# The order of the values in the last batch of an attention kernel with gated experts

## The chip, the cores and the metric

The kernel runs on one core of a Trainium2 chip. The metric is the device time of one execution in microseconds; each version is run several times and the median counts. One execution is also profiled, and from its trace come all the times of single instructions below.

## The reference

Two blocks follow one another. The first is a linear attention on features: for 4 batches, 4 heads, 1088 positions and 32 dimensions it makes 64 features of each key and query and divides a weighted sum of values by a sum of weights. Its result x (4 x 1088 x 128) goes to the second block, which holds nearly all of the time: four experts, each a causal softmax attention with a head of 64, of which every position takes the two with the largest gate.

```python
logits = x @ w_gate                      # top 2 of 4 experts, weights w
for e in range(E):                       # E = 4
    q = x @ wq[e]; k = x @ wk[e]; v = x @ wv[e]          # 1088 x 64
    scores = scale * (q @ k.transpose(0, 2, 1))          # causal mask
    a = np.exp(scores - scores.max(-1, keepdims=True))
    a /= a.sum(-1, keepdims=True) + 1e-09
    ye = a @ v @ wo[e]                                   # 1088 x 128
    out += mask[e] * w * ye
```

## The kernel before

The 1088 positions of a batch are nine tiles of 128 queries, the last of 64. The four experts are two groups g of two (e = 0, 1). One **unit** of work is one tile i of one group, and goes through these steps:

- `scores` (L416, L422): PE multiplies the queries of the tile with all keys up to it, for both experts, into PSUM banks of the pool `ps_sc`. It holds two tiles of two banks each; a tile over 512 columns wide takes one of them for each expert.
- DVE takes the maximum of each row (`mx`, L426 for tiles up to 512 columns, L429 else), ACT the exponential with the sum of the row (`soften`, L402), which writes `a` in SBUF. `a` has four buffers, so a pair of tiles with two experts fills them.
- `turns_of` (L476): PE transposes `a` in blocks of 128 by 128, up to four in a PSUM bank `tp`, and `evacuate` copies the bank to `aT` in SBUF (L72 on ACT, every third one L70 on DVE). The pool `ps_tp` has four banks, which all small products share.
- Two neighbouring tiles of a group are one pair p, with 256 queries. When both are turned, `values` (L546) multiplies `aT` with the values `vt`, block by block of keys (j), one product for each j and expert (two matmul instructions each in the trace), into one bank `av`.
- `gates` makes 1/sum times the gate weight (`r` on DVE L496 and L497, `rb` on POOL L500) and returns `turn`, which transposes `rb` on PE into the other half of the bank `av` (L506) and copies it to `rs` (L508, ACT). DVE multiplies the two (`yT`, L548).
- `output` (L599): PE multiplies `yT` of both groups with `wo`, a copy makes `ob`, and SP issues the output DMA (L604).

`units` yields the units of a batch, with their kind: "A" and "B" for the first and the second tile of a pair, "P" for a pair taken as one unit (both scores first, then all turns), "L" for the last tile of 64 queries. In the last batch (b = B - 1) the pairs come from the largest to the smallest, p = 3, 2, 1, 0, with the L unit behind p = 3; p = 1 is of kind P there, and p = 0 of kinds A and B.

PE's order is the order in which the program writes its instructions (`manual_schedule`); on the other engines a scheduler sets the order. For each unit the main loop writes: the scores (`make`); the values of an older group if one is `ready`; the jobs, which are the turns left over by the unit before and an output; and, for kinds A and B with more than two turns, the first half of its own turns. A group is ready one unit after it was closed:

```python
ready = len(groups) > (1 if kind != "L" and closed else 0)
```

So the values of a group stand behind the scores of a later unit. In batches 0 to 2 work of the next batch (`fill`) is spread between the jobs; the last batch has none. After the last unit come the turns left over, the values of the last group (p = 0, g = 1) with its gate, and the last output.

Of the kernel before, what the change touches and what calls it, by code (L numbers as in the profile page):

```python
# [10 lines left out]
F32 = mybir.dt.float32  # L11
BF16 = mybir.dt.bfloat16
I32 = mybir.dt.int32
ALU = mybir.AluOpType
# [5 lines left out]
def kernel(  # L20
# [20 lines left out]
    nc = tc.nc  # L41
    B, H, S, D = q.shape
    R = S1.shape[0]
    DM, E = w_gate.shape
    HD = wq.shape[2]
# [4 lines left out]
    NG = E // 2  # L50
# [73 lines left out]
    if NS == 2:  # L124
# [15 lines left out]
        def both(o, x, y, op):  # L140
            nc.vector.tensor_tensor(out=o, in0=x, in1=y, op=op)
# [326 lines left out]
    def turns_of(name, i, ats, aT, q0):  # L468

        def some(e0, e1, j0, j1):  # L470
            tp = ps_tp.tile([128, 512], F32, tag="tp", name=f"tp{name}_{e0}_{j0}")
            nk, nj = size(j0), j1 - j0
            for e in range(e0, e1):
                for j in range(j0, j1):
                    x = 128 * (nj * (e - e0) + j - j0)
                    nc.tensor.transpose(tp[0:nk, x : x + 128], ats[e][:, 128 * j : 128 * j + nk], ident)  # L476
            evacuate(aT[0:nk, e0:e1, j0:j1, q0 : q0 + 128],
                     tp[0:nk, 0 : 128 * nj * (e1 - e0)].rearrange("p (e j s) -> p e j s", e=e1 - e0, j=nj))

        n = min(i + 1, NJ - 1)  # L480
        if n <= 2:
            cuts = [(0, 2, 0, n)]
        elif n <= 4:
            cuts = [(0, 1, 0, n), (1, 2, 0, n)]
        elif n <= 6:
            cuts = [(0, 1, 0, 4), (0, 2, 4, n), (1, 2, 0, 4)]
        else:
            cuts = [(0, 1, 0, 4), (0, 1, 4, n), (1, 2, 0, 4), (1, 2, 4, n)]
        if i == NJ - 1:
            cuts.append((0, 2, n, NJ))  # L490
        return [lambda c=c: some(*c) for c in cuts]

    def gates(name, z, gws, w):

        r = p4.tile([128, w // 128, 2], F32, tag="r", name=f"r{name}")
        nc.vector.tensor_scalar_add(r, z, 1e-9)  # L496
        nc.vector.reciprocal(r, r)  # L497
        rb = p4.tile([128, 2, 128], F32, tag="rb", name=f"rb{name}", bufs=2)
        wide = [128, w // 128, 2, HD]
        nc.gpsimd.tensor_tensor(out=rb[:, 0 : w // 128].rearrange("p x (e d) -> p x e d", d=HD),  # L500
                                in0=gws[:, :, :, None].to_broadcast(wide), in1=r[:, :, :, None].to_broadcast(wide),
                                op=ALU.mult)

        def turn(t):
            for x in range(w // 128):
                nc.tensor.transpose(t[:, 128 * x : 128 * x + 128], rb[:, x], ident)  # L506
            rs = p4.tile([128, 256], F32, tag="rs", name=f"rs{name}", bufs=2)
            nc.scalar.copy(rs[:, 0:w], t[:, 0:w])  # L508
            return rs

        return turn
# [5 lines left out]
    def spend(us):  # L517

        debt[0] += us
        while fill and debt[0] >= fill[0][0] / 2:  # L520
            cost, f = fill.popleft()
            debt[0] -= cost
            f()
# [4 lines left out]
    def units(b, qk, vt, gw, gw8):  # L528


        for p in range((NJ - 1) // 2) if b < B - 1 else reversed(range((NJ - 1) // 2)):
            yT = p2.tile([128, NG, 256], F32, tag="yT", name=f"yT{b}_{p}")
            nk = 2 * (2 * p + 2)
            for g in range(NG):
                aT = p2.tile([128, 16 * 256], F32, tag="aT", name=f"aT{b}_{p}_{g}")
                aT = aT[:, 0 : nk * 256].rearrange("p (e j s) -> p e j s", e=2, s=256)
                z = p4.tile([128, 2, 2], F32, tag="z", name=f"z{b}_{p}_{g}")
                name = f"{b}_{p}_{g}"

                def values(to_gate, p=p, g=g, aT=aT, yT=yT, name=name):  # L540
                    av = ps_tp.tile([128, 512], F32, tag="tp", name=f"av{name}")
                    for j in range(2 * p + 2):
                        lo = 128 * max(0, j - 2 * p)
                        for e in range(2):
                            c = HD * (2 * g + e)
                            nc.tensor.matmul(av[HD * e : HD * e + HD, lo:256], vt[:, j, c : c + HD],  # L546
                                             aT[:, e, j, lo:256], start=(j == 0), stop=(j == 2 * p + 1))
                    nc.vector.tensor_tensor(out=yT[:, g], in0=av[:, 0:256], in1=to_gate(av[:, 256:]), op=ALU.mult)  # L548
                    return (lambda: output(b, p, yT)) if g == NG - 1 else None

                def close(p=p, g=g, z=z, name=name, values=values):
                    return gates(name, z, gw[:, 2 * p : 2 * p + 2, 2 * g : 2 * g + 2], 256), values

                def both(g=g, z=z, p=p):
                    return [scores(b, 2 * p + x, g, qk, z[:, x]) for x in range(2)]

                def turns(made, p=p, aT=aT, name=name):
                    return [f for x in range(2) for f in turns_of(f"{name}_{x}", 2 * p + x, made[x], aT, 128 * x)]

                if p == 1 or p == 0 and b < B - 1:  # L560
                    yield "P", both, turns, close
                    continue
                for x in range(2):
                    i = 2 * p + x
                    yield ("AB"[x], lambda i=i, g=g, z=z, x=x: scores(b, i, g, qk, z[:, x]),
                           lambda ats, i=i, aT=aT, x=x, name=name: turns_of(f"{name}_{x}", i, ats, aT, 128 * x),
                           close if x else None)
            if p == NJ // 2 - 1:
                yield last_unit(b, qk, vt, gw8)
# [37 lines left out]
    with tc.manual_schedule(engines={mybir.EngineType.PE}):  # L607

        warm = ps_tp.tile([128, 512], F32, tag="tp", name="warm")
        for _ in range(16):  # L610
            nc.tensor.matmul(warm[:, 0:128], idle, idle, start=True, stop=True)
        now, ahead, _, own = prepare(0)
        for _, f in ahead:
            f()

        turns, groups, closed, done = [], collections.deque(), False, None
        for b in range(B):
            if b + 1 < B:

                coming, ahead, mid, rest = prepare(b + 1)  # L620
                own, tail = own[:-5], own[-5:]
                lead = sum(c for c, _ in own)
                if b == 0:
                    own += tail
                    own += sum(ahead, [])
                else:
                    for f, o in zip(ahead, (tail[0:1], tail[1:2], tail[2:3], tail[3:])):
                        own += f + o
                fill.extend(own + mid)
                share = (sum(c for c, _ in fill) - lead) / sum(STEPS)  # L630
            for n, (kind, make, turned, close) in enumerate(units(b, *now)):
                jobs, turns = turns, []
                if done:
                    jobs.append(done)
                    done = None
                if kind == "L":
                    for f in jobs:
                        f()
                    jobs = []

                ready = len(groups) > (1 if kind != "L" and closed else 0)
                made = make()
                if ready:
                    to_gate, values = groups.popleft()
                    done = values(to_gate)
                us = share * STEPS[n] + (lead if n == 0 else 0.0) if b + 1 < B else 0.0
                gaps = max(len(jobs), 2)
                for s in range(gaps):
                    if s < len(jobs):
                        jobs[s]()  # L650
                    spend(us / gaps)
                turns = turned(made)
                if len(turns) > 2 and kind in "AB":
                    for f in turns[: len(turns) // 2]:
                        f()
                    turns = turns[len(turns) // 2 :]
                closed = close is not None
                if close:
                    groups.append(close())
            spend(1e9)  # L660
            debt[0] = 0.0
            now, own = coming, rest
        for f in turns + ([done] if done else []):
            f()
        for to_gate, values in groups:
            done = values(to_gate)
        done()
# [30 lines left out]
```

## Time and profile before

| | |
|---|---|
| median of 4 runs | 409.06 us (407.7 to 411.1) |
| profiled execution, its own time | 411.1 us |
| its span | 409.3 us |
| PE busy | 388.6 us, 95% of the span |
| DVE, ACT, POOL busy | 231.9, 224.1, 58.9 us |
| mean granted clock of PE | 0.992 |
| last batch, from its first scores | 317.25 us to the end |

The span is counted from the first instruction to the end of the last, with the last DMA. A line of the timeline gives the start, the time for which the instructions of the line were busy, engine and line of the code, the operation, the tiles out and in, their shapes and how many there were; what stands in brackets is the idle time of the engine before it and what ended it. PEld is the load of weights for a matmul. The chain that ended last gives start, length and what ran.

### The profile page before, as it was taken

The page shows a single profiled execution, that of the slowest core. Times are in us where ns is not written, and L with a number is a line of the kernel's source. Part 1 is how long each engine was busy: PE and PEld are TensorE (multiplying, and loading weights), DVE is VectorE, ACT ScalarE, POOL GpSimd, SP SyncE. Part 2 cuts the span into 40 slices and gives each one's busy share as a digit, 9 for nine tenths or more (in the row PEclk, how much of TensorE's full clock was granted, in tenths as well). Part 3 has the DMA queues.
Part 4 walks back from the last instruction along what each step waited for, and adds up shares of the span by engine and source line. Part 5 has one row for each costly group of instructions (what it writes and reads, how often), then busy time and mean ns, then how long its engine had stood idle before and what let it go on. Part 6 is the DMA issues. An engine that isn't in the chain of part 4 may idle for free.

```text
span 409.3 us, 8453 instructions
## 1 busy us (share of the span) xinstructions
PE 388.6 (95%) x3424; PEld 281.3 (69%) x3424; DVE 231.9 (57%) x501; ACT 224.1 (55%) x566; POOL 58.9 (14%) x92
## 2 busy tenths in 40 slices
PE   8899999999999999999999999999999989998895
PEld 8775787776748677776756778776665666675583
DVE  6877865565465564556446554645654555456332
ACT  2246565556555656556656466646654464656343
POOL 4400550000004340000002530000000000000100
PEclk9999999999999999999999999999999999999889
DMA  8604112000000000000000000000000000000000
GB/s 200 181 14 151 57 57 69 13 2 14 0 3 14 3 2 14 14 1 2 13 2 2 14 5 2 13 14 0 14 2 0 16 3 1 2 14 3 2 14 27
DMA packets 11351, 9.99 MB, mean 24 GB/s; under 512 B 3632, under 2 KB 10288, under 8 KB 11312
## 3 DMA queue, kind: packets, MB, share of 16 engines
q1 hardware_dynamic: 11296, 9.44, 8.3%
q8 instruction: 27, 0.44, 0.5%
q14 instruction: 12, 0.10, 0.1%
q10 hardware_dynamic: 16, 0.00, 0.0%
HBM read 7.22 MB, written 2.23 MB: 23 GB/s over the span
## 4 chain that ended last, share of the span: by engine, by line
PE 76%; DVE 11%; ACT 7%; issue 2%; DMA 1%; POOL 1%; SPq 0%; ACTq 0%; POOLq 0%
PE sc L416 17%; PE tp L476 16%; PE av L546 12%; PE qk L332 6%; ACT a L402 5%; PE po L599 4%; PE num L306 3%; PE vg L344 3%; PE av L584 3%; PE av L506 3%; DVE mx L458 2%; DVE mx L429 2%; PE sc L442 2%; PE kv L283 2%; PE tq L296 2%
## 5 line engine op out<-in xcount | busy, mean ns | idle before, releaser
L402 ACT ACTIVATE a<-sc,mx 128x1024 f32<-128x1024 f32 (+7 forms) x136 | 103.3, 765 | 72.4 <-DVE mx L429 47.2
L476 PE MATMUL tp<-ident,a 128*128 128x128 f32 (+1 forms) x648 | 92.7, 278 | 2.6 <-ACT a L402 1.4
L429 DVE TENSOR_REDUCE mx<-sc 128x1 f32<-128x640 f32 (+3 forms) x64 | 62.6, 1020 | 42.0 <-PE sc L422 42.0
L416 PE MATMUL sc<-qkT 64*128 64x512 f32 (+3 forms) x384 | 80.8, 519 | 2.2 <-ACT a L402 2.2
L476 PEld LDWEIGHTS tp<-ident,a 128*128 128x128 f32 (+1 forms) x648 | 74.0, 143 | 12.4 <-ACT a L402 3.0
L72 ACT COPY aT<-tp 128x512 f32<-128x512 f32 (+3 forms) x122 | 65.2, 553 | 30.1 <-PE tp L476 29.5
L546 PE MATMUL av<-aT,vt 128*64 128x256 f32 (+1 forms) x640 | 70.9, 369 | 2.3 <-ACT aT L72 2.3
L500 POOL TENSOR_TENSOR rb<-gw,r 128x256 f32<-128x256 f32 (+1 forms) x36 | 21.2, 590 | 305.0 <-DVE r L497 188.6
L546 PEld LDWEIGHTS av<-aT,vt 128*64 128x64 f32 x640 | 43.7, 139 | 23.5 <-ACT aT L72 2.7
L70 DVE COPY aT<-tp 128x512 f32<-128x512 f32 (+3 forms) x58 | 36.1, 624 | 34.5 <-PE tp L476 34.5
L416 PEld LDWEIGHTS sc<-qkT 64*128 64x128 f32 x384 | 33.8, 186 | 29.4 <-issue 21.6
L508 ACT COPY rs<-av 128x256 f32<-128x256 f32 (+1 forms) x36 | 13.0, 361 | 40.7 <-PE av L506 40.3
L332 PE MATMUL qk<-xT,wqk 128*128 128x512 f32 x64 | 31.4, 603 | 1.6 <-ACT a L402 1.6
L426 DVE TENSOR_REDUCE mx<-sc 128x2 f32<-128x256 f32 (+3 forms) x32 | 25.5, 816 | 7.6 <-PE sc L422 7.2
L402 ACT ACTIVATION_READ_ACCUMULATOR a<-sc,mx 128x1 f32 x136 | 27.3, 201 | 0.0
L422 PEld LDWEIGHTS <-mpick 64*128 64x128 bf16 x256 | 13.9, 95 | 17.4 <-issue 12.9
L599 PE MATMUL po<-wo,yT 128*128 128x128 f32 (+1 forms) x144 | 20.5, 282 | 1.9 <-DVE yT L548 0.8
L344 PE MATMUL vg<-wvg,xT 128*128 128x260 f32 (+1 forms) x72 | 20.3, 393 | 1.8 <-DVE r L496 0.6
L496 DVE TENSOR_SCALAR r<-z 128x4 f32<-128x4 f32 (+1 forms) x36 | 7.3, 204 | 23.9 <-ACT a L402 22.4
L72 ACT COPY qkT<-qk 128x512 f32<-128x512 f32 x23 | 13.5, 589 | 13.3 <-PE qk L332 13.0
L599 PEld LDWEIGHTS po<-wo,yT 128*128 128x128 f32 (+1 forms) x144 | 17.3, 185 | 4.4 <-DVE aT L70 1.3
L306 PE MATMUL num<-kvz,qpT 128*128 128x66 f32 x144 | 17.8, 272 | 0.6 <-ACT aT L72 0.3
(122 smaller groups left out, 412.7 us busy)
## 6 DMA issues: line engine op xcount, KB each, us to landing
kin<-in_k_dram SPq DMA_DIRECT2D x4, 544.0 KB, 3.9
qin<-in_q_dram SPq DMA_DIRECT2D x4, 544.0 KB, 6.0
vin<-in_v_dram SPq DMA_DIRECT2D x16, 128.0 KB, 5.5
out_dram<-ob SPq DMA_DIRECT2D x16, 128.0 KB, 1.8
vtl<-in_v_dram SPq DMA_DIRECT2D x8, 16.0 KB, 3.6
wqk<-in_moe_wq_dram SPq DMA_DIRECT2D x1, 128.0 KB, 5.0
wqk<-in_moe_wk_dram SPq DMA_DIRECT2D x1, 128.0 KB, 3.2
wvg<-in_moe_wv_dram SPq DMA_DIRECT2D x1, 128.0 KB, 3.1
```

What stands on the lines that cost most here:

```text
L70: nc.vector.tensor_copy(out_, in_)
L72: nc.scalar.copy(out_, in_)
L306: nc.tensor.matmul(num[:, 66 * (y - 2 * x0) : 66 * (y - 2 * x0) + 66], qpT[:, y], kvz[:, y % 2].rearrange("p h d -> p (h d)"), start=True, ...
L332: nc.tensor.matmul(t, wt(a), xT[:, 512 * c : 512 * c + 512], start=True, stop=True)
L344: nc.tensor.matmul(t[0:m, 0 : E * HD + E], xT[:, 128 * j : 128 * j + m], wvg, start=True, stop=True)
L402: nc.scalar.activation(out=dst, in_=src, func=ACTF.Exp, bias=mx, accum_out=z)
L416: nc.tensor.matmul(sc[e][:, c0:c1], qk[rows, g, 128 * i : 128 * i + 128], qk[rows, NG + g, c0:c1], start=True, stop=(c1 < n))
L426: nc.vector.tensor_reduce(mx, t[:, :, 0:n], axis=AX.X, op=ALU.max, negate=True)
L429: nc.vector.tensor_reduce(mx[:, e : e + 1], sc[e][:, 0:n], axis=AX.X, op=ALU.max, negate=True)
L476: nc.tensor.transpose(tp[0:nk, x : x + 128], ats[e][:, 128 * j : 128 * j + nk], ident)
L546: nc.tensor.matmul(av[HD * e : HD * e + HD, lo:256], vt[:, j, c : c + HD], aT[:, e, j, lo:256], start=(j == 0), stop=(j == 2 * p + 1))
L599: nc.tensor.matmul(po[0:nq, DM * x : DM * x + DM], yT[:, g, 128 * x : 128 * x + nq], wo_sb[:, g], start=(g == 0), stop=(g == NG - 1))
```

## The change

All of it is in the last batch. (1) For kinds A behind a B, the first half of the values (j up to p + 1) of the group just closed is written behind the jobs and ahead of the unit's own turns; the second half stands where all of them stood. This is so for the groups p = 3, g = 0 and p = 2, g = 0. (2) For kind P, the values of the group just closed, all of them, are written in the unit that follows it, behind the jobs, which are that group's last turns. (3) p = 0 becomes a pair of kind P too, and takes its tile 1 before its tile 0, in scores and turns. (4) For the last group `rb` is made on DVE instead of POOL, and the gate's transposes and `rs` are written ahead of the values.

```diff
-    def gates(name, z, gws, w):
+    def gates(name, z, gws, w, last=False):
...
-        nc.gpsimd.tensor_tensor(out=rb[:, 0 : w // 128].rearrange("p x (e d) -> p x e d", d=HD),
-                                in0=gws[:, :, :, None].to_broadcast(wide), in1=r[:, :, :, None].to_broadcast(wide),
-                                op=ALU.mult)
+        (nc.vector if last else nc.gpsimd).tensor_tensor(
+            out=rb[:, 0 : w // 128].rearrange("p x (e d) -> p x e d", d=HD),
+            in0=gws[:, :, :, None].to_broadcast(wide), in1=r[:, :, :, None].to_broadcast(wide), op=ALU.mult)
...
-                def values(to_gate, p=p, g=g, aT=aT, yT=yT, name=name):
-                    av = ps_tp.tile([128, 512], F32, tag="tp", name=f"av{name}")
-                    for j in range(2 * p + 2):
+                av = []
+
+                def some_values(j0, j1, p=p, g=g, aT=aT, name=name, av=av):
+                    if not av:
+                        av.append(ps_tp.tile([128, 512], F32, tag="tp", name=f"av{name}"))
+                    for j in range(j0, j1):
...
+                def values(to_gate, half=False, p=p, g=g, yT=yT, av=av, some_values=some_values):
+                    if half:
+                        return some_values(0, p + 1)
+                    if b == B - 1 and p == 0 and g == NG - 1:
+                        av.append(ps_tp.tile([128, 512], F32, tag="tp", name="av"))
+                        rs = to_gate(av[0][:, 256:])
+                        some_values(0, 2)
+                    else:
+                        some_values(p + 1 if av else 0, 2 * p + 2)
+                        rs = to_gate(av[0][:, 256:])
+                    nc.vector.tensor_tensor(out=yT[:, g], in0=av[0][:, 0:256], in1=rs, op=ALU.mult)
...
+                order = (1, 0) if b == B - 1 and p == 0 else (0, 1)
+
+                def both(g=g, z=z, p=p, order=order):
+                    return {x: scores(b, 2 * p + x, g, qk, z[:, x]) for x in order}
...
-                if p == 1 or p == 0 and b < B - 1:
+                if p <= 1:
                     yield "P", both, turns, close
...
+                if b == B - 1 and closed and kind in "AP" and n:
+                    to_gate, values = groups[-1]
+                    if kind == "P":
+                        groups.pop()
+                        done = values(to_gate)
+                    elif last_kind != "L":
+                        values(to_gate, half=True)
                 turns = turned(made)
...
-                closed = close is not None
+                closed, last_kind = close is not None, kind
```

More of the change, by code (lines that the diff above doesn't have):

```diff
@@ L545, in values @@
                             c = HD * (2 * g + e)
-                            nc.tensor.matmul(av[HD * e : HD * e + HD, lo:256], vt[:, j, c : c + HD],
+                            nc.tensor.matmul(av[0][HD * e : HD * e + HD, lo:256], vt[:, j, c : c + HD],
                                              aT[:, e, j, lo:256], start=(j == 0), stop=(j == 2 * p + 1))
-                    nc.vector.tensor_tensor(out=yT[:, g], in0=av[:, 0:256], in1=to_gate(av[:, 256:]), op=ALU.mult)
+                def values(to_gate, half=False, p=p, g=g, yT=yT, av=av, some_values=some_values):
[9 more added lines that the diff above has]
+                    nc.vector.tensor_tensor(out=yT[:, g], in0=av[0][:, 0:256], in1=rs, op=ALU.mult)
@@ L549, in values @@
                     return (lambda: output(b, p, yT)) if g == NG - 1 else None
                 def close(p=p, g=g, z=z, name=name, values=values):
[L552 to L558, printed above, removed]
@@ L560, in units, with turns @@
-                if p == 1 or p == 0 and b < B - 1:
+                    return gates(name, z, gw[:, 2 * p : 2 * p + 2, 2 * g : 2 * g + 2], 256,
+                                 b == B - 1 and p == 0 and g == NG - 1), values
+                order = (1, 0) if b == B - 1 and p == 0 else (0, 1)
+                def both(g=g, z=z, p=p, order=order):
+                    return {x: scores(b, 2 * p + x, g, qk, z[:, x]) for x in order}
+                def turns(made, p=p, aT=aT, name=name, order=order):
+                    return [f for x in order for f in turns_of(f"{name}_{x}", 2 * p + x, made[x], aT, 128 * x)]
```

## The prediction

> **What bounds the kernel now.** I read the page first (engine busy rows, clock row), then the busy time in stretches, the chain that ended last, and the timeline of the last batch. PE is busy 388.6 of 409.3 us and the chain is 76% PE, so a change of order can only win back PE's idle time and slow time. The edits touch only the last batch, which begins near 317 us. Busy time per stretch of 3.41 us (column two is length and PE's busy time, then PEld, DVE, ACT, POOL; then granted clock, DMA share, GB/s):
>
> ```profile
> 372.05:375.46 3.41, 3.41 (x31) 2.28 (x30) 2.86 (x6) 1.59 (x6) 0.61 (x1) 1.00 0.00 0
> 375.46:378.87 3.41, 1.72 (x14) 0.90 (x13) 1.85 (x4) 2.95 (x9) 0.00 (x0) 1.00 0.00 0
> 378.87:382.28 3.41, 3.41 (x18) 1.56 (x16) 1.25 (x2) 0.00 (x0) 0.61 (x1) 0.50 0.02 5
> ...
> 385.70:389.11 3.41, 1.70 (x20) 1.17 (x20) 1.39 (x4) 2.32 (x8) 0.61 (x1) 1.00 0.00 0
> 389.11:392.52 3.41, 3.41 (x21) 2.74 (x18) 0.42 (x1) 1.18 (x5) 0.00 (x0) 0.50 0.00 0
> ...
> 402.76:406.17 3.41, 2.40 (x18) 1.70 (x18) 0.43 (x1) 0.54 (x3) 0.17 (x1) 1.00 0.00 0
> ```
>
> Twice PE is idle for half of a stretch (1.72 and 1.70 us busy), and each time the granted clock is 0.50 for the next 3.41 us; with 2.40 us busy the clock kept 1.00. In a slow stretch the 24 values matmuls took 3.60 us against 2.60 at full clock, the four 512-wide scores 1.72 against 1.11, and 14 turns 2.55 against about 1.6. Each slow stretch costs 1.7 us: first 0.6 + 1.0 + 0.1; second 0.56 (16 values) + 0.25 (gate) + 0.95 (turns). What makes PE idle there:
>
> ```profile
> 375.99 1.07 ACT L72 COPY aT<-tp 128x512 f32<-128x512 f32 x2
> ...
> 376.15 0.92 PE L416 MATMUL sc<-qkT 64*128 64x384 f32 x4 [0.36 <-ACT a L402]
> ...
> 376.93 0.72 ACT L402 ACTIVATE a<-sc,mx 128x512 f32<-128x512 f32 x1
> ...
> 378.46 1.72 PE L416 MATMUL sc<-qkT 64*128 64x512 f32 x4 [1.34 <-ACT a L402]
> ...
> 384.59 0.58 ACT L402 ACTIVATE a<-sc,mx 128x384 f32<-128x384 f32 x1
> ...
> 387.05 0.98 ACT L72 COPY aT<-tp 128x384 f32<-128x384 f32 x2
> ...
> 388.08 2.29 PE L546 MATMUL av<-aT,vt 128*64 128x256 f32 x16 [1.65 <-ACT aT L72]
> ```
>
> The first stall is a score bank not yet read by ACT's exponentials; the second is the copy of turned tiles to aT, queued on ACT behind four exponentials. Those exponentials began only at 384.59, because a pair uses all four buffers of `a` and the turns that free them stood behind 24 values. The last chain:
>
> ```profile
> 402.82 0.87 PE av L546 x8
> 403.70 0.38 PE av L506 x2
> ...
> 404.15 0.38 ACT rs L508
> ...
> 404.56 0.44 DVE yT L548
> ...
> 405.04 0.95 PE po L599 x6
> ...
> 406.01 0.37 ACT ob L72
> ```
>
> After it 2.92 us pass until the span ends (the last output DMA).
>
> **Part 1: the halves.** For the groups p=3 g=0 and p=2 g=0, half of the values moves from behind the next scores to ahead of the next unit's own turns, where PE waits now:
>
> ```profile
> 332.54 1.09 PE L476 MATMUL tp<-ident,a 128*128 128x128 f32 x8
> ...
> 333.67 0.59 ACT L72 COPY aT<-tp 128x512 f32<-128x512 f32 x1 [2.20 <-PE tp L476]
> ...
> 334.64 0.68 DVE L70 COPY aT<-tp 128x512 f32<-128x512 f32 x1
> ...
> 335.31 0.98 PE L476 MATMUL tp<-ident,a 128*128 128x128 f32 x7 [1.09 <-ACT a L402]
> ```
>
> No instruction is added: 16 and 12 matmuls move. The half reads the block j 0 to 3, e=1, which is the first of the two tiles turned at 332.54. Its copy is the one on DVE, behind two maxima, and ends at 335.33. So the second matmul of the half waits until 335.35, the gap is not filled, and the half (16 at 1.67/16) ends near 336.95. Seven turns then reach 337.72, where the next scores begin (336.22 now): the softmax of tile 7 is 1.5 us late. PE has 1.67 us less to do behind those scores, so the turns catch up with ACT: its second exponential ends near 343.35 (341.9 now), and rs, yT and the copies follow it. The scores of tile 8 start at 344.85 to 345.3 instead of 344.53. I take +0.5; bounds 0 (ACT places rs between the two exponentials) and +1.5 (the whole shift passes on). Group p=2 g=0: copies end at 366.43, the 12 matmuls (1.25 us) fill little, scores of tile 5 end 0.95 later, PE itself reaches the next pair 0.4 us earlier, but ACT's copies keep their time: 0, between -0.4 and +0.5.
>
> **Part 2: pairs' values behind their turns.** Full-clock prices per piece, start to start: scores of 384, 512, 256 and 128 columns 0.81, 1.10, 0.69 and 0.48; a turn 0.109; values of 24, 16, 8 matmuls 2.52, 1.67, 0.80; gate 0.28; an output 0.99. On ACT: exponential of 512, 384, 256, 128 columns 0.70, 0.57, 0.46, 0.36; copies of 512 and 384 columns 0.59 and 0.48, of 256 columns 0.40. Every third copy is DVE's. Without the shift of part 1:
> - p=1 g=0: both scores and eight turns end at 375.35 (0.4 early). Values of p=2 g=1 now stand here and need both copies of 375.99 to 377.06: idle 1.7, start 377.05. With the gate, 379.85.
> - p=1 g=1: scores to 381.75, no bank stall (the banks were read by 378.3). Fourteen turns to 383.3. The output's bank waits for a DVE copy behind the maxima: 383.9, then 0.99: 384.9. The copies for the next values: if ACT does them ahead of the exponentials of the second tile, as at 375.99, they end at 384.6; if after, as at 387.05, near 386.0. The unit is like the first row (the second maximum not ready): 384.9. Values and gate: 386.85.
> - p=0 g=0: two scores 388.05, fourteen turns 389.6. From 388.55, when the first tile is turned, ACT has four exponentials (1.65) and three copies (1.66) before the last block of aT is there: 391.9, an idle 2.3 us. Values and gate: 393.85.
> - p=0 g=1: scores 395.0, six turns 395.7, output 396.7; ACT from 395.4 has 1.65 + 0.40: 397.5, idle 0.8. Values and gate 398.6.
>
> A wait ahead of values now blocks the next scores too, so the next maximum and exponentials are late by as much; this is counted, as each line starts where the last ended. SP only issues the outputs, each 0.4 us, with nothing behind it. The order "smaller last" shortens the last exponentials to 0.36 us each.
>
> **Part 3: the end.** Six turns 399.25, last gate 399.55; the 512-wide copy on DVE ends at 399.85 to 400.6, I take 400.25. The last rb moves from POOL (0.61) to DVE; nearest row there is yT's 0.44. Its r is ready near 397.6, so it lies behind the values and turns; uncovered it costs 0.4. Values end 401.1, yT 401.6 (the gate's turn and rs, 403.70 to 404.56 now, are off the path: 0.8 saved), po 402.6, ob 403.0, plus 2.92: **405.95**. With part 1: 406.45.
>
> **The clock.** The waits of 1.7 and 2.3 us are as long as those that cost a slow stretch; 0.8 is not. Stretches are 3.41 us on a fixed grid, so a wait cut by the grid may escape. I count one slow stretch: 406.45 + 1.7 = 408.15. The Trainium skill (TensorE: Matmul & The Clock Gate, "HAM oscillation — how this bites in real kernels") says that only PE gaps above about 3.4 us drop the clock; the two rows of 0.50 after gaps below 1.7 us contradict it. By that rule no wait of the new order would cost clock, and the sum would be 406.45.
>
> **Scale.** The profiled execution took 411.1 us, 1.8 more than its span, and it is the slowest of four runs (407.7 to 411.1, median 409.06). With two slow stretches of 1.7 us in it, the lowest run would be one without any, 411.1 - 3.4, and the median one with about one; that is inferred. So 408.15 + 1.8 = 409.95, about **409.9 us**, stands against the median: +0.2%, no change (1% is about what can be told apart here). The old idle of 1.7 and 1.65 us is traded for 1.7, 2.3 and 0.8 in new places, less 0.8 at the end.
>
> **Rivals.**
> - *ACT's copies go ahead of its exponentials everywhere* (0.2). For it: the order at 375.99. Against it: 387.05. The 2.3 us shrink to about 1.05 and the 0.8 to 0.1; part 1 costs nothing, no slow stretch: 405.95 - 1.25 - 0.7 + 1.8 = 405.8 us. Below 405.0, a real gain, needs part 1 to save as well.
> - *The clock decides* (0.15): three stretches at half speed, behind the waits at 375.35, 384.9 and 389.6. It comes to this when the copies ahead of the p=1 g=0 values end after 386. 406.45 + 3 x 1.7 + 1.8 = 413.4 us, slower by 1.1%. Two stretches give 411.7, still within 1%. Against it: 2.40 us busy kept the clock.
> - *The half's bank is held too long* (0.1): av of p=3 g=0 keeps one of four PSUM banks from 334.3 to yT near 344. If the second tile turned after the gate must wait for that bank, PE stops at 342.1: +1.2 us, 411.1 us. Against it: two tiles that are already copied lie free.
>
> The forecast itself has 0.55; its own range is 408 to 411.5. The 8-in-10 range takes in most of the first two rivals: 406.0 to 412.9. Faster by over 1%: 0.07, the lower part of the first rival. Slower by over 1%: 0.10. Within: 0.83.
>
> **What would show it.** PE still idle about 1.1 us ahead of the first half, released by DVE's aT; scores of tile 7 about 1.5 us later; no wait of scores for ACT's `a` in the pairs; values waiting for ACT's aT ahead of p=2 g=1 (1.7 us) and p=1 g=1 (2.3 us), each perhaps followed by a stretch at 0.50; the last yT straight behind the last values. Wrong if PE waits under 0.5 us ahead of those values, or if the first half starts by 334.4.

## The result and the profile after

The changed kernel takes 409.65 us (median of 53 runs, 409.32 to 410.22) against 409.16 us for the kernel before (79 runs, 407.35 to 411.31). The ratio is 1.0021 with an interval of [1.0013, 1.0029]: no change by the 1% of the prediction. What changed most is the spread. The runs of the kernel before lie in three groups: 39 at 407.35 to 408.49, 34 at 409.16 to 410.12, 6 at 410.84 to 411.31. The 91 runs of the same kernel that were measured beside the experiments fall into three such groups, and their granted clock is listed: 0.998 to 1.00, 0.994 to 0.996 and 0.992. All 53 runs after are one group, with a clock of 0.998 to 1.00. So the change takes away the half-speed stretches (1.6 us each, in half of the runs) and pays for it: it is 1.8 us slower than the kernel before without them (about 407.85).

The profiled execution after took 409.58 us with a span of 407.7; it reaches the first edit 0.20 us earlier than the one before (scores at 330.57 instead of 330.77).

**The halves.** The timeline after, where 334.64 and 335.31 stood:

```profile
334.44 0.68 DVE L70 COPY aT<-tp 128x512 f32<-128x512 f32 x1
...
335.18 1.94 PE L549 MATMUL av<-aT,vt 128*64 128x256 f32 x14 [0.73 <-DVE aT L70]
...
337.96 1.99 PE L416 MATMUL sc<-qkT 64*128 64x512 f32 x8
...
343.45 1.66 PE L476 MATMUL tp<-ident,a 128*128 128x128 f32 x12 [0.18 <-DVE aT L70]
...
345.05 1.95 PE L442 MATMUL sc<-qkT 64*64 64x512 f32 x16
```

Two of the 16 matmuls run at 333.85; the other 14 wait for DVE's copy. With the 0.20 us of offset added, the scores of tile 7 (337.96, 336.22 before) are 1.9 us late and those of tile 8 (345.05, 344.53 before) 0.7.

**The pairs.** The two largest of PE's waits before, in the last batch (total, times, longest):

```profile
PE av L546 <- ACT aT L72: 2.3, 2, 1.6
PE sc L416 <- ACT a L402: 2.2, 4, 1.3
```

The four largest after, from 330 us on, and the timeline of the two longest single ones:

```profile
PE av L549 <- ACT aT L72: 3.0, 4, 1.1
PE av L549 <- DVE r L497: 1.5, 1, 1.5
PE av L549 <- DVE aT L70: 1.5, 2, 0.7
PE sc L416 <- ACT a L402: 0.5, 2, 0.3
```

```profile
385.55 0.98 ACT L72 COPY aT<-tp 128x384 f32<-128x384 f32 x2
...
386.58 1.74 PE L549 MATMUL av<-aT,vt 128*64 128x256 f32 x16 [1.11 <-ACT aT L72]
...
392.27 1.09 ACT L72 COPY aT<-tp 128x512 f32<-128x512 f32 x2
...
392.93 2.21 PE L549 MATMUL av<-aT,vt 128*64 128x256 f32 x16 [1.51 <-DVE r L497]
```

The bank stall of the scores in the pairs is gone; nearly all that PE waits for is a copy to aT ahead of values: in the pairs 0.75 at 377.67, 1.11, 1.51 and 0.87 at 399.13. The wait of 1.51 is put down to DVE's r, but two copies of ACT end at about 392.86 and at 393.36, and behind them start two and 14 of the 16 weight loads, at 392.93 and 393.42.

The idle time understates two of these waits, because some matmuls run in the middle of them. The 24 values of p=2 g=1 take from 376.28 to their gate at 380.19, 3.91 us, where 2.52 us is the price without a wait: the wait costs 1.4 us. At p=1 g=1 the turns end at 391.42 and the gate starts at 395.08, 3.66 us, where the 16 values need 1.67: 2.0 us.

**The clock.** Three stretches of 3.41 us. Their grid is known because the clock falls once in this execution too, at 406.63, behind the last work; the stretches are counted back from there.

```profile
375.91:379.32 3.41, 2.66 (x23) 1.53 (x22) 0.89 (x3) 3.06 (x10) 0.00 (x0) 1.00 0.00 0
...
389.56:392.97 3.41, 1.90 (x23) 1.61 (x17) 1.82 (x5) 2.67 (x11) 0.00 (x0) 1.00 0.01 2
392.97:396.39 3.42, 3.42 (x34) 2.20 (x34) 0.43 (x2) 0.77 (x2) 0.61 (x1) 1.00 0.00 0
```

The emptiest of the pairs has 1.90 us of PE, and the next one keeps 1.00. Wherever a stretch of this length is laid between 330 and 403 us, it holds at least 1.90 us of PE in this execution; in the one before, the least was 1.70.

**The end**, as the chain after shows it: the last values no longer have a gate's turn and rs behind them.

```profile
401.24 0.61 DVE aT L70
...
401.98 0.89 PE av L549 x8
...
402.96 0.44 DVE yT L562
...
403.44 0.95 PE po L617 x6
...
404.41 0.37 ACT ob L72
```

### The profile page after: what moved, and what is told of

It is laid out like the page before. It is cut to its first block, busy times and chain, and to the rows that moved or that the text cites. A ratio compares the mean times of both kernels' runs of the same rounds, so it can differ in the third digit from the quotient of the medians.

```text
span 407.7 us, 8457 instructions
## 1 busy us (share of the span) xinstructions
PE 387.2 (95%) x3424; PEld 279.2 (68%) x3424; DVE 232.5 (57%) x502; ACT 222.7 (55%) x566; POOL 58.3 (14%) x91
## 4 chain that ended last, share of the span: by engine, by line
PE 75%; DVE 12%; ACT 7%; issue 3%; DMA 1%; POOL 1%; SPq 0%; ACTq 0%; POOLq 0%; DVEq 0%
PE sc L416 17%; PE tp L476 15%; PE av L549 13%; PE qk L332 6%; ACT a L402 5%; PE po L617 4%; PE num L306 3%; DVE mx L429 3%; PE vg L344 3%; PE av L602 3%; PE av L506 3%; DVE mx L458 2%; PE sc L442 2%; PE kv L283 2%; PE tq L296 2%
## 5 line engine op out<-in xcount | busy, mean ns | idle before, releaser
L476 PE MATMUL tp<-ident,a 128*128 128x128 f32 (+1 forms) x648 | 91.7, 276 | 1.3 <-DVE aT L70 1.0
L476 PEld LDWEIGHTS tp<-ident,a 128*128 128x128 f32 (+1 forms) x648 | 72.9, 141 | 11.5 <-issue 3.3
L416 PE MATMUL sc<-qkT 64*128 64x512 f32 (+3 forms) x384 | 79.1, 516 | 0.5 <-ACT a L402 0.5
L549 PE MATMUL av<-aT,vt 128*64 128x256 f32 (+1 forms) x640 | 72.1, 363 | 6.0 <-ACT aT L72 3.0
L562 DVE TENSOR_TENSOR yT<-av,rs 128x256 f32<-128x256 f32 x32 | 13.3, 417 | 12.6 <-ACT rs L508 11.4
```

What stands on the lines that cost most here:

```text
L416: nc.tensor.matmul(sc[e][:, c0:c1], qk[rows, g, 128 * i : 128 * i + 128], qk[rows, NG + g, c0:c1], start=True, stop=(c1 < n))
L549: nc.tensor.matmul(av[0][HD * e : HD * e + HD, lo:256], vt[:, j, c : c + HD], aT[:, e, j, lo:256], start=(j == 0), stop=(j == 2 * p + 1))
```

## The experiments

"Group without a slow stretch" means the runs with a granted clock of 0.997 or more; for the kernel before they centre on 407.7 to 407.9 in all the comparisons, taken as 407.85 below.

**The halves alone.** From the changed kernel, parts 2 to 4 undone; of the edit, the place of the values:

```diff
-                if b == B - 1 and closed and kind in "AP" and n:
+                if b == B - 1 and closed and kind == "A" and last_kind == "B" and n in (2, 7):
                     to_gate, values = groups[-1]
-                    if kind == "P":
-                        groups.pop()
-                        done = values(to_gate)
-                    elif last_kind != "L":
-                        values(to_gate, half=True)
+                    values(to_gate, half=True)
```

> The kernel before with part 1 alone (both halves, nothing else). My theory, from the trace of the changed kernel: the half waits for DVE's copy to aT, so the gap is not filled, the next softmax is late, and the halves cost about 0.75 us; the runs without a half-speed stretch should lie near 408.5 instead of 407.8, and the profile should show the scores of tile 8 about 0.7 us later. Rival: the halves fill PE's old gaps of 1.09 and 0.28 us, which part 2 then loses again: runs without a half-speed stretch near 406.6.

Measured: ten of twelve runs at 408.50 to 409.03, two at 410.1 and 410.3 (clock 0.996); ratio 1.0005 [0.9986, 1.0025] over all. The group without a slow stretch is 0.8 us above that of the kernel before, and the profile shows the second part of the half waiting 0.74 us for DVE's aT. The halves cost; the rival falls.

**Without the halves.** The `elif last_kind != "L"` branch removed from the changed kernel.

> The changed kernel without part 1 (values of p=3 g=0 and p=2 g=0 whole, as before). My theory: 0.75 us faster than the changed kernel, 408.9 us, all runs in one narrow group, PE idle ahead of the pairs' values unchanged (0.75, 1.1, 1.5, 0.9 us). Rival (the halves pay): 410.9 us.

Measured: 409.19 us (408.59 to 409.67), one group; waits of 0.75, 1.11, 1.52 and 0.86. The halves cost 0.46 here: the direction holds, and the size is below the 0.75 expected.

**The end alone.** In the kernel before, `rb` of the last group on DVE and its gate ahead of its values.

> The kernel before with part 4 alone: rb of the last group on DVE, its gate ahead of its values; p=0 stays two units. My theory: the gate's turn and rs leave the last chain, 0.5 to 0.8 us less: runs without a half-speed stretch near 407.2 us, and the three groups of times of the kernel before stay, 1.7 us apart. Rival: rb on DVE comes later than the copies of the last turns, and PE waits for it ahead of the values: no change, 407.8.

Measured: 408.31 to 408.65 in three runs, the others 409.0 to 410.7 with clocks of 0.989 to 0.996; ratio 1.0018 [0.9996, 1.004]. My theory falls: the group without a slow stretch, of three runs only, is 0.6 to 0.8 us slower. The timeline of this run shows why:

```profile
401.46 0.41 PE L506 MATMUL av<-ident,rb 128*128 128x128 f32 x2 [0.79 <-DVE rb L500]
...
402.38 0.87 PE L548 MATMUL av<-aT,vt 128*64 128x256 f32 x8 [0.52 <-ACT rs L508]
```

PE waits for rb, which on DVE stands behind the yT of the group before, and then the values wait for rs. The rival named the first wait, not the second. With p=0 as a pair, rb is made early (from 399.41 in the changed kernel), and both are covered by the last turns and their copy; in the run with parts 3 and 4 alone (below), where the last turns come ahead of the values of p=0 g=0, the wait of 0.52 us for rs is there again.

**Matmuls of zeros in the two old waits.** In the kernel before:

```diff
+    def keep_warm(name, n):
+        t = ps_tp.tile([128, 512], F32, tag="tp", name=f"warm{name}")
+        for _ in range(n):
+            nc.tensor.matmul(t[:, 0:128], idle, idle, start=True, stop=True)
...
+                        if b == B - 1 and p == 1 and g == 1 and x:
+                            keep_warm("1", 11)
...
+                    if b == B - 1 and n == 11:
+                        keep_warm("2", 13)
```

> The kernel before with matmuls of zeros, whose product is not used, in its two long PE waits: 11 ahead of the second scores of p=1 g=1, 13 ahead of the values of p=1 g=0; the waits themselves stay. My theory: the half-speed stretches come from those waits; with PE busy there the clock keeps 1.00 in every run and all runs lie near 407.8, none above 408.7. Rival: the spread of the kernel before (407.4 to 411.3) has another cause, or matmuls of zeros do not count as activity: the three groups of times stay, and the median is 409.2 or, with the added work in the way, higher.

Measured: 410.62 us, eleven runs at 410.24 to 411.11 and one at 411.97. Each product ran as two matmuls, 2.72 and 3.17 us in all, so they overran the waits by 2.9 us, and 407.85 + 2.9 = 410.75. The number expected was wrong by this; the spread does shrink, though the one run at 411.97 has a clock of 0.996. So again, to fit:

> As the run with matmuls of zeros, which lasted 2.7 and 3.2 us where the waits last 1.4 and 1.65, but with 5 and 6 of them (1.25 and 1.5 us), so that they fit into the waits. My theory: no run has a half-speed stretch and all lie between 407.4 and 408.6, median 407.9, against a median of 409.3 for the kernel before. Rival: the clock depends on something else; the times stay in three groups up to 411.

Measured: 407.76 us, all twelve runs at 407.36 to 408.16, clock 0.997 to 1.00; ratio 0.9965 [0.9945, 0.9986]. Its busy time in stretches, where the clock of the kernel before was 0.50 from 378.87 on:

```profile
375.00:379.00 4.00, 3.61 (x28) 2.61 (x28) 2.40 (x4) 3.48 (x10) 0.00 (x0) 1.00 0.00 0
379.00:383.00 4.00, 4.00 (x40) 2.66 (x36) 1.24 (x2) 0.35 (x1) 0.61 (x1) 1.00 0.02 4
```

Work that is thrown away saves 1.0 us in the mean (407.78 against 408.78 for the 29 runs beside it), and only by taking the upper two groups away: the three groups are the clock, and the clock is those two waits.

**Part 2 alone** (for p=1; no halves, p=0 and the end as before).

> The kernel before with part 2 alone for p=1 (values of p=2 g=1 and of p=1 g=0 behind their turns; no halves; p=0 stays two units, its order and the last gate as before). Theory from the trace of the changed kernel: the old waits of 1.70 and 1.65 us are replaced by 0.75, 0.3 and 1.1, and the values of p=1 g=1 stand behind a score again: runs without a half-speed stretch near 406.7 (1.1 below the kernel before), with few or no slow stretches. So part 2 pays and part 3 takes it back. Rival: part 2 is what costs; 408.9 or more.

Measured: 407.55 us (407.02 to 408.05), one group; ratio 0.9961 [0.9943, 0.9979]. It gains 0.3 without a slow stretch (0.25 against the runs beside it), not 1.1, and keeps the clock, which is most of what it saves in the mean. The theory's sign holds, its size does not, in part because it counted the wait ahead of p=2 g=1 with the idle time of 0.75 us, where it costs 1.4.

**Parts 3 and 4 alone** (the values where they stood).

> The kernel before with parts 3 and 4 alone (p=0 a pair with its tile 0 last, last gate first on DVE; values stand where they stood; no halves). Theory: the waits of 1.70 us in the scores of p=1 stay, the values of p=1 g=0 get 0.7 us more cover, but the values of p=1 g=1 and p=0 g=0 wait for ACT, which has four exponentials and three copies: lowest group near 408, with half-speed stretches in part of the runs. Rival: the pair and the shorter end pay by themselves, lowest group near 406.5.

Measured: ten runs at 406.88 to 407.66, two near 408.93 (clock 0.995); ratio 0.9969 [0.9948, 0.999]. 0.5 faster than the kernel before without a slow stretch: between the two expectations, and the sign of my theory was wrong.

So part 2 alone gains 0.3 and parts 3 and 4 alone 0.5, and together (without halves) they lose 1.3. They meet in one place: with p=0 a pair of kind P, the rule of part 2 also puts the values of p=1 g=1 and p=0 g=0 right behind their turns. That was tested by itself, in the changed kernel without the halves:

```diff
-                    if kind == "P":
+                    if kind == "P" and n < 11:
                         groups.pop()
                         done = values(to_gate)
-                    elif last_kind != "L":
-                        values(to_gate, half=True)
```

> The changed kernel without the halves, and with the rule of part 2 for the values of p=2 g=1 and p=1 g=0 only: those of p=1 g=1 and p=0 g=0 stand behind the next scores and the output, as before. Theory: the 1.3 us by which parts 2, 3 and 4 together are slower, though part 2 and parts 3 and 4 alone gain 0.3 and 0.5, are the waits of 1.5 and 0.9 us ahead of those two values, where the pair p=0 gives ACT four exponentials with nothing behind them on PE. So 407.2 us, about 2 below the run without halves. Rival: the interaction lies elsewhere (the last gate, the order of p=0); 408.7 or more.

Measured: 407.58 us (407.21 to 407.86), one group; ratio 0.9966 [0.9948, 0.9985]. 1.6 us below the run without halves (2.0 expected). The waits of 1.5 and 0.9 ahead of those two values are gone, less what comes back: 0.32 for a score bank and 0.27 for the last turns. So this place is most of the interaction, and not all of it: the parts alone gain 0.8 in sum, here they gain 0.3, and the 0.5 between stays open.

**Eight buffers for the exponentials' tiles**, in all batches (`bufs=8` on the tag "a"), in the changed kernel and in the kernel before:

> The changed kernel with eight buffers for the exponentials' tiles, nothing else. Theory: the waits ahead of values are ACT's, and four buffers make the exponentials late; with eight the wait of 1.1 us ahead of the values of p=1 g=0 shrinks to about 0.5, and that of 1.5 us stays, as its exponentials wait for maxima: 408.9 us. Rival: the buffers set all the waits: 407 or less.

> The kernel before with eight buffers for the exponentials' tiles, nothing else. Theory: the exponentials of p=1 g=1 run during the values of p=2 g=1, so the copies behind the turns are at once done and the wait of 1.65 us ahead of the values of p=1 g=0 goes; the wait of 1.34 us for the score bank stays, so half-speed stretches come only from it: lowest group 406.2, at most two groups. Rival: no change (407.8), as the exponentials then stand in front of something else.

Measured: the changed kernel 407.87 us (eleven runs at 407.56 to 408.41, one at 409.25; ratio 0.9977 [0.9959, 0.9994]), 1.8 us less than with four: more than the theory's 0.75, and short of the rival. The wait ahead of the values of p=1 g=0 is gone, where 0.5 was expected to stay, and the one ahead of p=1 g=1 is still 1.45. The kernel before 407.09 us: three runs at 405.46 to 406.22, seven at 406.74 to 407.73 with a clock of 0.995 to 0.996, and none with two slow stretches; ratio 0.9945 [0.9922, 0.9969]. Its timeline: an exponential of p=1 g=1 now runs at 377.93 (384.59 before), ACT copies at once behind the turns, and the wait of 1.65 is gone; the one for the score bank stays and still costs a slow stretch in most runs.

```profile
377.93 0.61 ACT L402 ACTIVATE a<-sc,mx 128x384 f32<-128x384 f32 x1
378.12 1.87 PE L416 MATMUL sc<-qkT 64*128 64x512 f32 x4 [1.34 <-ACT a L402]
...
384.53 1.02 ACT L72 COPY aT<-tp 128x384 f32<-128x384 f32 x2 [0.28 <-PE tp L476]
...
385.88 2.10 PE L546 MATMUL av<-aT,vt 128*64 128x256 f32 x16
```

**A version that uses all of this.** No halves; p=0 a pair; eight buffers; and in the last batch values stand where PE would wait, behind work that is ready:

```diff
+                if b == B - 1 and n >= 9:
+                    def oldest():               # the values of the oldest group
...
+                    if n == 10:
+                        made = make(oldest)     # between the two scores
+                    else:
+                        made = make()
+                    if n == 11:
+                        done()                  # output of p=2
+                        oldest()
+                    for f in jobs:                               # turns left over
+                        f()
+                    if n == 12:
+                        oldest()
```

At the end the last group's gate stands ahead of the values of p=0 g=0.

> A new order from these readings, no halves: eight buffers for the exponentials' tiles instead of four (in all batches); in the last batch the values of p=2 g=1 stand between the two scores of p=1 g=1, those of p=1 g=0 behind the scores of p=0 g=0 and an output, those of p=1 g=1 behind the scores of p=0 g=1 and the turns of p=0 g=0; the last gate is made ahead of the values of p=0 g=0. Theory (PE waits ahead of values because ACT's copies stand behind exponentials that wait for buffers): nearly all waits covered, no slow stretch, 403 to 404.5 us. Rival: ACT is the bound in this stretch whatever the order: 407 or more.

> The combined order with four buffers for the exponentials' tiles, as in the kernel before. Theory: the order makes most of the gain of 4.3 us, and the buffers let ACT do the exponentials of p=1 g=1 and p=0 ahead of the turns: 404.8 us. Rival: the buffers are all of it, in all four batches: 407 or more, or none of it: 403.5.

Measured: 403.54 us with eight buffers (six runs, 403.21 to 404.01; ratio 0.9857 [0.9827, 0.9887]), 404.45 with four (404.13 to 404.80; 0.9882 [0.9855, 0.991]). Faster than both kernels. The order makes 3.4 us against 407.85 and the buffers 0.9. No values wait any longer; PE's waits with eight buffers, from 330 us on:

```profile
PE sc L416 <- ACT a L402: 1.6, 4, 0.9
PE tp L476 <- ACT a L402: 1.3, 2, 1.1
```

## Why the prediction was right, and where it was not

The forecast of no change came true (409.9 us forecast, 409.65 measured). Right were the reading of the spread before, the cost of the halves in kind, and three of the four places where values wait in the pairs; the wait ahead of p=1 g=0 was missed. That the number came so near is luck: two terms of the sum were wrong, one by +1.25 us and one by -1.7, and they nearly cancel.

- **Part 1, +0.5**: right in kind. The half waits for the copy on DVE, tile 8 is 0.7 late; the halves alone cost 0.8, and 0.46 inside the changed kernel. I had the second matmul of the half waiting; it is the third (each product is two matmuls). By its letter this met one of my signs of being wrong, a half that starts by 334.4: two of its matmuls ran at 333.85. The other 14 started at 335.18, where I had 335.35.
- **Part 2, the order on ACT at p=1 g=1**: wrong end chosen. I took the copies ahead of the second tile's exponentials, as at 375.99; ACT did all four exponentials first, as at 387.05, which I had priced at 1.1 more (copies done near 386.0 instead of values at 384.9). The values start at 386.58 (385.4 forecast with part 1), behind a wait of 1.11 that my sum put at nothing.
- **Part 2, the other waits**: idle times of 0.75 instead of 1.7 ahead of p=2 g=1, 1.51 instead of 2.3 ahead of p=1 g=1, 0.87 instead of 0.8 ahead of p=0 g=0. The chain is nearer to my sum than the idle times are, as matmuls that find their block run inside two of the waits: they cost 1.4 and 2.0. The gate of p=2 g=1 stands at 380.19, forecast 380.07 with part 1.
- **The sum without a slow stretch**: 406.45 forecast, span 407.7. Of the difference of 1.25, 1.1 is the choice on ACT; the rest is in small pieces.
- **The clock, +1.7**: wrong. I counted one slow stretch as the likeliest; none of 53 runs has one. I set idle waits of 1.7 and 2.3 us beside those before; the profile shows 0.75 and 1.51 us of idle time there, and no stretch of the pairs with less than 1.90 us of PE. That this is why the clock held is likely and not shown, as busy time alone does not tell which stretches are followed by a slow one (last section).
- **Scale**: inferred there, shown here. The three groups of runs, 1.5 to 1.7 us apart, are zero, one and two slow stretches; the zeros in the waits remove the upper two.
- **The end, 0.8 saved**: the chain is as forecast, but it is not a gain of part 4. Alone it loses 0.6 to 0.8. Its trace says that it needs the pair with tile 0 last, which makes r early; part 3 was not run without part 4, so what each is worth in the pair is not known.
- **The rivals**: copies ahead of exponentials everywhere did not come (385.55 stands behind all four); the clock did not decide; the half's bank was no stop (turns paused 0.18 us at 343.45).

What the prediction did not see is that parts 2 and 3 meet: each pays alone. It priced the 2.3 and 0.8 us as the cost of part 2, and did not ask whether they belonged to one part or to the pair of them.

## What to carry to other kernels

Putting a consumer right behind its producer on the busiest engine exposes the whole way through the other engines, here 0.75 to 1.5 us of idle time at each place; with ready work in between, no values wait, as the version with 403.54 us shows. Ask for each moved step what the engine behind it will be doing at that moment, and try the parts of a change alone and in pairs, as their costs need not add. When times of one kernel fall in groups, look at the clock before explaining them by the code: here a wait of 1.3 to 1.7 us cost about as much again, 1.6 us, in the runs in which the clock fell behind it. And price a wait by the start of the work before and behind it, as the idle time alone can be too small.

## What the hardware showed that I had not expected

The clock fell to 0.50 for 3.41 us behind stretches in which PE was busy 1.70, 1.72 and (end alone) 1.73 us, and kept 1.00 behind 1.76 (end alone, and halves alone) and 1.90 (changed kernel). But it also fell behind a stretch with 1.78 us busy (kernel before with eight buffers, 374.96 to 378.37) and, at the end of the run with the end alone, behind one with 2.03. So busy time as the profile counts it is not quite what decides, and where the limit lies was not settled. Matmuls of zeros were enough to keep the clock: all twelve runs that had them to fit stayed at 0.997 or more.
